# A decode kernel: VectorE and ScalarE given a hardware loop as TensorE has, row sums taken with the exponentials, GpSimd given two layout steps, and the gather and transpose of O moved

## The chip, the cores and the metric

The kernel runs on one core of one Trainium2 chip; the other cores do nothing. The metric is the device time of one execution in microseconds (us), lower is better. Every run named here is of the fast state, and most kernels repeat within about 0.5 us; where one does not, the text says so. Beside each experiment the kernel before was run on the same chip.

## The reference, cut to what matters

The program is one decode step of a gated mix. Branch A is attention over a cache for 8 sequences and 32 heads, branch B a small MLP. All data are bfloat16.

```python
# A: x (8,1,576), k_cache and v_cache (8, 32, 4096, 128), wq (576, 4096), wo (4096, 576)
q = (x @ wq) -> (8, 32, 1, 128)
p = softmax(q . k_cache / sqrt(128))          # over 4096 positions
a = (p . v_cache) -> (8, 1, 4096) @ wo
# B: layernorm, 576 -> 4608, gelu, 4608 -> 576
g = sigmoid(sum(x * gate_w));  return g * a + (1 - g) * b
```

The caches are 537 MB together. With weights 557 MB must be read, and each cache byte is used once.

## The kernel before

The work is cut into 32 groups g, each of one sequence and eight heads. A group needs one K load and one V load of 8.39 MB each (128 partitions with 64 KB each). SBUF holds three such slots, so a load may start when an earlier one has been used up. Per group:

- VectorE multiplies K by q in eight chunks, in place (`mult`); TensorE adds up 16-wide pieces by products with the identity; VectorE reduces what is left (`reduce`).
- VectorE finds the maximum (`softmax`), ScalarE takes the exponentials into P, VectorE adds P up (`rowsum`).
- TensorE multiplies P by V (`pv`), ScalarE copies the result out (`evict`), TensorE gathers it (`gather`), VectorE divides by the sum (`norm`). Every third group TensorE transposes three results (`turn`).

TensorE's groups 2 to 31 are a hardware loop of ten turns with three groups in each. The other engines have all instructions written out. The parts that matter for the argument:

```python
# ... cut: set-up, weights, MLP
    def load_kv(kind, g):                      # one 8.39 MB load, issued from SyncE
        ...
        land[kind, g] = op("sync", lambda e: e.dma_start(slot[s][:, :, :], src), free[n - 3], ...)
# ...
    def rowsum(g):                             # 128x2048 -> 128x1 on VectorE
        v_rs[g] = op("vector", lambda e: e.tensor_reduce(
            out=rr[:, :], in_=P[:, :, :].rearrange("p h t -> p (h t)"), axis=AX.X, op=ALU.add),
            [a_exp[g], p_z.get(g - 1)])
# ...
    for g in range(NG):
        if g >= G0 and place(g) == 0:
            S.mark()                           # a turn of TensorE's loop starts
        def between(c, g=g):                   # called between the eight chunks c of scores(g)
            if g >= G0:
                if c == 1:
                    gather(g - 2)
                if c == 3:
                    norm(g - 2)
                if c == 4 and place(g) == GL - 1:
                    turn((g - 2) // GL)
            if g >= 1 and c == 3:
                rowsum(g - 1)
            if c == 5:
                q_of(g + 1)
        scores(g, between)
        free[n_of["k", g]] = [p_sum[g, NCK - 1]]   # K's slot is free after the last score sum
        next_load()                            # ... the last group loads wo instead
        if g >= 1:
            pv(g - 1)
            free[n_of["v", g - 1]] = [p_pv[g - 1]]
            next_load()
        softmax(g)                             # contains the exponentials
        if g >= 1:
            evict(g - 1)
# ... cut: the last group's O, the product with wo, the output
```

Each freed K slot takes a V load and each freed V slot a K load. The last K slot takes wo.

## Time and profile before

| | before |
|---|---|
| time, median | 1305.18 us (1304.88 to 1305.40, 3 runs) |
| bytes read | 557 MB |
| share of the 16 DMA engines' span used by the load queue | 99.3% |
| VectorE, TensorE, ScalarE busy | 68%, 61%, 12% |
| a cache load lands after the one before | 19.35 us, mostly (433 GB/s) |
| last V lands; last piece of wo lands; end of span | 1287.4; 1298.7; 1302.5 us |

From the profile page of the kernel before: the engines' busy time, share and instructions; the row of DMA shares in 40 slices and the rate in each; then the queues with packets, MB and share of 16 engines' span.

```profile
PE 795.1 (61%) x5186; PEld 355.3 (27%) x5186; DVE 881.6 (68%) x885; ACT 150.0 (12%) x363; POOL 3.4 (0%) x19
DMA  9999999999999999999999999999999999999997
GB/s 393 436 439 419 427 437 433 429 433 435 431 433 433 437 429 441 429 439 431 433 433 423 435 423 443 425 431 439 425 439 429 437 431 423 445 421 441 429 435 297
q1 hardware_dynamic: 11200, 556.93, 99.3%
q14 instruction: 10, 0.08, 0.0%
```

The DMA engines are the resource that is full. Queue 14 brings instructions: only 0.08 MB, whose share rounds to nothing.

From the same page, four groups of instructions (count, busy us, mean ns of one, idle time before them and its cause):

```profile
L503 DVE TENSOR_TENSOR SL<-SL,q_bc 128x4096 bf16<-128x4096 bf16 x256 | 581.7, 2283 | 216.8 <-DMA SL<-in_A_k_cache_dram 216.8
L551 DVE TENSOR_REDUCE rr<-P 128x1 f32<-128x2048 bf16 x32 | 72.9, 2278 | 0.3
L482 ACT ACTIVATE Qm<-Q,sel 128x256 bf16<-128x256 bf16 x33 | 16.3, 495 | 0.0
L511 PE MATMUL psb<-SL,ident 128*128 128x512 bf16 x2048 | 613.6, 459 | 468.1 <-DVE SL L503 467.5
```

VectorE waits 216.8 us for K loads. That is what its slack looks like: the row sums (L551) take 72.9 us of an engine that then waits.

The packet records of the trace give start, duration, size and queue of each DMA packet, but not its engine. As every engine runs almost without a break, a packet belongs to the engine whose last packet ended where it starts. Worked out so, the end of each engine's last cache packet is (us, sorted):

```
before: 1281.7 1281.7 1281.7 1281.7 1281.8 1281.9 1281.9 1282.0 1282.1 1282.1 1282.1 1282.1 1282.3 1282.3 1283.6 1286.9
```

One of the 16 is 5 us behind the typical one. A load counts as landed when all 16 engines have finished their part.

### The profile page before, as it was taken

How to read it: one execution, taken by the hardware profiler on the slowest of the kernel's cores; microseconds unless marked ns; L12 is line 12 of the kernel's file. 1: busy time of each engine (PE TensorE's matmuls, PEld its weight loads, DVE VectorE, ACT ScalarE, POOL GpSimd, SP SyncE). 2: the span in 40 equal slices, each digit the busy share in tenths (PEclk: the TensorE clock that was granted, in tenths of full speed). 3: DMA queues.
4: the chain of work that ended last, by engine and by line, in shares of the span. 5: the costliest groups of instructions: out<-in, count | busy, mean ns of one | idle time of the engine just before them, and what ended most of it. 6: DMA issues, size and time to landing. Idle time of an engine off the chain costs nothing.

```text
span 1302.5 us, 11916 instructions
## 1 busy us (share of the span) xinstructions
PE 795.1 (61%) x5186; PEld 355.3 (27%) x5186; DVE 881.6 (68%) x885; ACT 150.0 (12%) x363; POOL 3.4 (0%) x19
## 2 busy tenths in 40 slices
PE   2467476656667466567557556656557566557556
PEld 1323232223223122223223222223223122223224
DVE  3388577766668576668666667766668676667754
ACT  1011110111110111100111110111110011110011
POOL 1000000000000000000000000000000000000000
PEclk8599786887797787888787797887798788788788
DMA  9999999999999999999999999999999999999997
GB/s 393 436 439 419 427 437 433 429 433 435 431 433 433 437 429 441 429 439 431 433 433 423 435 423 443 425 431 439 425 439 429 437 431 423 445 421 441 429 435 297
DMA packets 11411, 557.27 MB, mean 428 GB/s; under 512 B 1360, under 2 KB 1376, under 8 KB 2816
## 3 DMA queue, kind: packets, MB, share of 16 engines
q1 hardware_dynamic: 11200, 556.93, 99.3%
q8 instruction: 9, 0.15, 0.0%
q10 hardware_dynamic: 192, 0.11, 0.0%
q14 instruction: 10, 0.08, 0.0%
HBM read 557.03 MB, written 0.01 MB: 428 GB/s over the span
## 4 chain that ended last, share of the span: by engine, by line
DMA 55%; DVE 25%; PE 18%; issue 0%; ACT 0%; SPq 0%
DMA SL<-in_A_k_cache_dram 54%; DVE SL L503 18%; PE psb L511 13%; PE psb L565 5%; DVE s_sb L516 4%; DVE rr L551 3%; DMA SL<-in_A_wq_dram 1%; DVE Orow L584 0%; PE psb L403 0%; ACT P L546 0%; PE psb L578 0%; PE psb L454 0%; DVE OT L599 0%; PE psb L593 0%; DVE rz L583 0%
## 5 line engine op out<-in xcount | busy, mean ns | idle before, releaser
L511 PE MATMUL psb<-SL,ident 128*128 128x512 bf16 x2048 | 613.6, 459 | 468.1 <-DVE SL L503 467.5
L503 DVE TENSOR_TENSOR SL<-SL,q_bc 128x4096 bf16<-128x4096 bf16 x256 | 581.7, 2283 | 216.8 <-DMA SL<-in_A_k_cache_dram 216.8
L511 PEld LDWEIGHTS psb<-SL,ident 128*128 128x128 bf16 x2048 | 215.8, 114 | 833.7 <-DVE SL L503 547.3
L516 DVE TENSOR_REDUCE s_sb<-psb 128x32 f32<-128x512 f32 x256 | 175.6, 686 | 109.6 <-PE psb L511 109.4
L546 ACT ACTIVATE P<-s_sb,hb 128x256 bf16<-128x256 f32 x256 | 105.5, 494 | 301.0 <-PE psb L565 255.9
L565 PE MATMUL psb<-SL,P 128*32 128x512 bf16 x2048 | 119.9, 386 | 0.0
L492 ACT ACTIVATE q_bc<-psb 128x128 bf16<-128x128 f32 x32 | 8.9, 278 | 804.4 <-PE psb L486 804.4
L565 PEld LDWEIGHTS psb<-SL,P 128*32 128x32 bf16 x2048 | 91.1, 168 | 28.3 <-issue 13.1
L551 DVE TENSOR_REDUCE rr<-P 128x1 f32<-128x2048 bf16 x32 | 72.9, 2278 | 0.3
L578 PE MATMUL psb<-O_sb,sel 128*8 128x128 f32 x256 | 33.9, 276 | 4.6 <-ACT O_sb L570 4.6
L599 DVE CAST OT<-psb 128x8 bf16<-128x8 f32 x32 | 3.7, 187 | 37.0 <-PE psb L593 37.0
L578 PEld LDWEIGHTS psb<-O_sb,sel 128*8 128x8 f32 x256 | 21.7, 93 | 8.3 <-ACT O_sb L570 4.8
L570 ACT ACTIVATE O_sb<-psb 128x512 f32<-128x512 f32 x32 | 18.4, 575 | 6.0 <-PE psb L565 6.0
L482 ACT ACTIVATE Qm<-Q,sel 128x256 bf16<-128x256 bf16 x33 | 16.3, 495 | 0.0
L425 DVE TENSOR_TENSOR SL<-psb,SL 104x384 f32<-104x384 f32 x3 | 1.7, 553 | 18.7 <-PE psb L421 18.7
L534 DVE TENSOR_REDUCE mA<-s_sb 128x1 f32<-128x256 f32 x32 | 13.4, 420 | 1.1
L444 PE MATMUL psb<-ident,SL 8*32 8x8 bf16 x144 | 8.0, 195 | 7.3 <-DVE SL L435 7.3
L584 DVE TENSOR_SCALAR Orow<-psb,rz 8x128 bf16<-8x128 f32 x32 | 10.9, 340 | 1.1
L583 DVE RECIPROCAL rz<-psb 8x1 f32<-8x1 f32 x32 | 4.8, 149 | 10.1 <-PE psb L578 10.1
L444 PEld LDWEIGHTS psb<-ident,SL 8*32 8x32 bf16 x144 | 7.9, 148 | 7.7 <-DVE SL L435 7.7
L421 PE MATMUL psb<-SL 128*8 128x384 bf16 x60 | 5.0, 475 | 8.0 <-DMA SL<-in_B_w_dram 8.0
L486 PE MATMUL psb<-Qm,Sel 128*64 128x128 bf16 x66 | 8.6, 256 | 0.0
(72 smaller groups left out, 104.8 us busy)
## 6 DMA issues: line engine op xcount, KB each, us to landing
SL<-in_B_w_dram SPq DMA_DIRECT2D x1, 5184.0 KB, 38.4
SL<-in_B_w_dram SPq DMA_DIRECT2D x1, 4608.0 KB, 24.7
SL<-in_A_wq_dram SPq DMA_DIRECT2D x1, 4096.0 KB, 13.1
SL<-in_A_wo_dram SPq DMA_DIRECT2D x1, 2304.0 KB, 11.8
SL<-in_A_wo_dram SPq DMA_DIRECT2D x1, 1152.0 KB, 14.2
SL<-in_B_w_dram SPq DMA_DIRECT2D x1, 576.0 KB, 25.7
SL<-in_A_wo_dram SPq DMA_DIRECT2D x1, 576.0 KB, 15.0
SL<-in_A_wo_dram SPq DMA_DIRECT2D x2, 288.0 KB, 15.3
```

The lines of the kernel that those rows point to most:

```text
L444: p_hT = op("tensor", lambda e, o=o, i=i, c=c: e.matmul(o, lhsT=i, rhs=ident[32 * c:32 * c + B, 32 * c:32 * c + B], start=True, stop=True) ...
L482: t = op("scalar", lambda e: e.activation(out=Qm[:, :, :].rearrange("p k d -> p (k d)"), in_=Q4[:, 2 * hg * DH:(2 * hg + 2) * DH], func=AC ...
L503: v_mult[g, c] = op("vector", lambda e: e.tensor_tensor(out=part, in0=part, in1=qb, op=ALU.mult), [land["k", g], a_qb[g]], token=in_loop(g))
L511: p_sum[g, c] = op("tensor", lambda e, r=r, n=n: e.matmul(tr_ps[par][:, :], lhsT=ident[:, :], rhs=r, start=(n == 0), stop=(n == NCH - 1)), w)
L516: v_red[g, c] = op("vector", lambda e: e.tensor_reduce(out=s_sb[:, s, c * CT:(c + 1) * CT], in_=tr_ps[par][:, :].rearrange("p (t c) -> p t ...
L534: t = op("vector", lambda e: e.tensor_reduce(out=mA[:, 0:1], in_=s_sb[:, s, :], axis=AX.X, op=ALU.max), [v_red[g, NCK - 1], c_mA])
L546: a_exp[g] = op("scalar", lambda e, h=h: e.activation(out=P[:, h, :], in_=s_sb[:, s, :], func=ACT.Exp, bias=hb8[:, h:h + 1], scale=1.0), [ ...
L551: v_rs[g] = op("vector", lambda e: e.tensor_reduce(out=rr[:, :], in_=P[:, :, :].rearrange("p h t -> p (h t)"), axis=AX.X, op=ALU.add), [a_ ...
L565: p_pv[g] = op("tensor", lambda e, o=o, tq=tq: e.matmul(o, lhsT=P[:, :, :].rearrange("p h t -> p (h t)")[:, tq::NTQ], rhs=vb[:, tq::NTQ, : ...
L570: a_ev[g] = op("scalar", lambda e: e.activation(out=O_sb[:].rearrange("p t d -> p (t d)"), in_=o_ps[:, :], func=ACT.Copy), [p_pv[g], p_oz. ...
L578: p_oz[g] = op("tensor", lambda e, tt=tt: e.matmul(oz_ps[0:HB, 0:DH], lhsT=sel32[:, :, tt], rhs=O_sb[:, tt, :], start=(tt == 0), stop=(tt ...
L584: v_norm[g] = op("vector", lambda e: e.tensor_scalar(out=Orow[32 * (g % GL):32 * (g % GL) + HB, :], in0=oz_ps[0:HB, 0:DH], scalar1=rz[0:HB ...
```

## The change: intent and diff

VectorE and ScalarE each get a ten-turn loop like TensorE's, so that they too need no new instructions. The exponentials give their row sums themselves (`accum_out`), so VectorE's row sum goes. GpSimd prepares Qm (the next q, masked, which a product with `Sel` then spreads over the partitions) and places the transposed O. The gather of O, with its sums, and the transpose move to other places in the group, and a V slot is now free only after the eviction. The core of the diff:

```diff
+    LOOPED = ("tensor", "vector", "scalar")
...
+        i0, i1, n, turns = self.body(engine)
         for rec in ops[:i0]:
-            one(rec, False)
-        with eng.Fori(0, (i1 - i0) // n):
-            for rec in ops[i0:i0 + n]:
-                one(rec, True)
+            one(rec)
+        if turns:
+            body, back = self.loops[engine]
+            with eng.Fori(0, turns):
+                for rec, need, give in zip(ops[i0:i0 + n], body, back):
+                    for sem, val in need:
+                        eng.wait_ge(sem, val)
+                    done(rec, rec["fn"](eng))
+                    for sem, by in give:
+                        eng.sem_inc(sem, -by)
         for rec in ops[i1:]:
-            one(rec, False)
+            one(rec)
... (q_of: Qm moves from ScalarE to GpSimd)
-        t = op("scalar", lambda e: e.activation(
-            out=Qm[...], in_=Q4[...], func=ACT.Copy, scale=sel32[...]), ...)
+        g_qm[g] = op("gpsimd", lambda e: e.tensor_scalar(
+            out=Qm[...], in0=Q4[...], scalar1=sel32[...], scalar2=None, op0=ALU.mult), ...)
... (the exponentials give their sums)
+    def exps(g):
         for h in range(HB):
             a_exp[g] = op("scalar", lambda e, h=h: e.activation(
-                out=P[:, h, :], in_=s_sb[:, s, :], func=ACT.Exp, bias=hb8[:, h:h + 1], scale=1.0),
+                out=P[:, h, :], in_=s_sb[:, :], func=ACT.Exp, bias=hb8[:, h:h + 1], scale=1.0,
+                accum_out=acc[:, place(g), h:h + 1]),
...
-    def rowsum(g):
-        v_rs[g] = op("vector", lambda e: e.tensor_reduce(...))
... (the transposed O: one copy on VectorE, then GpSimd)
+    def stage(k):
+        v_st[k] = op("vector", lambda e: e.tensor_copy(out=OTs[:, :, :, :], in_=tp_of), [p_tp[k], g_ot.get(k - 1)])
+    def place_o(k):
+        for g in range(GL * k, min(GL * k + GL, NG)):
+            g_ot[k] = op("gpsimd", lambda e, ...: e.tensor_copy(out=OT[:, 2 * hg:2 * hg + 2, :, b], in_=OTs[:, :, :, g % GL]), [v_st[k]])
... (the order within a group)
-            if g >= G0:
-                if c == 1:
-                    gather(g - 2)
-                if c == 3:
-                    norm(g - 2)
-                if c == 4 and place(g) == GL - 1:
-                    turn((g - 2) // GL)
-            if g >= 1 and c == 3:
-                rowsum(g - 1)
-            if c == 5:
+            if c == 1:
                 q_of(g + 1)
+            if in_loop(g) and place(g) == 0:
+                if c == 2:
+                    turn(k, True)
+                if c == 4:
+                    stage(k)
         scores(g, between)
-        free[n_of["k", g]] = [p_sum[g, NCK - 1]]
+        if in_loop(g):
+            if place(g) == 0 and k >= 0:
+                place_o(k)
+            gather(g - 2)
+        free[n_of["k", g]] = [p_z[g - 2] if in_loop(g) else p_sum[g, NCK - 1]]
...
         if g >= 1:
             pv(g - 1)
-            free[n_of["v", g - 1]] = [p_pv[g - 1]]
-            next_load()
         softmax(g)
+        if in_loop(g):
+            norm(g - 2)
+        exps(g)
         if g >= 1:
             evict(g - 1)
+            free[n_of["v", g - 1]] = [a_ev[g - 1]]
+            next_load()
```

## The prediction

> **What bounds the kernel now: the DMA engines.** The page's queue table puts the load queue at 99.3% of all 16 engines' span, at 428 GB/s on average. The Trainium skill ("DMA: Bandwidth & Descriptors", Specifications) gives a fabric ceiling of 435 GB/s; the landings agree: a typical 8.39 MB cache load lands 19.35 us after the one before, or 433 GB/s. VectorE is 68% busy, TensorE 61%, ScalarE 12%. In the timeline K's slot is given back 6 to 11 us before the load in flight lands, so the queue doesn't run dry: VectorE's 39 us turn has about 11 us of slack.
>
> **What the change removes and adds.** Row sum on VectorE (2.28 us a group, 72.9 us in all): gone. Qm (0.5 us) goes from ScalarE to GpSimd. All inside slack, so worth nothing. A K slot comes back about 2 us sooner; a V slot about 4 us later (after the exps, 3.3 us, and the eviction, 0.58 us), when another 19 us load is still queued behind the one in flight, so that costs nothing either.
>
> **The one thing that reaches the bound: instruction fetch.** Queue 14 in the trace's packet records brings 8192 bytes at 58.8, 238.1, 406.0, 588.1, 778.5, 972.9 and 1145.6 us: about 128 VectorE instructions apart (885 in 1300 us is about 27 a group of 39 us). Each holds up one DMA engine: the next 64 KB packet takes about 3.07 us instead of 2.42, after a 0.3 us gap, so about 0.97 us. The loads landing at 412, 607, 782, 977 and 1152 us indeed came after 20.3 to 20.4 us instead of 19.35. All hit the same engine: at the end 14 of the engines have finished the last V between 1281.7 and 1282.3 us, one only at 1286.9, so V lands at 1287.4 and the last piece of wo at 1298.7. That engine is the critical path.
>
> With VectorE looping, fetches end after the first turn of the loop: the two early ones stay, five go, 5 x 0.97 = 4.8 us, which brings the late engine level with the rest. The Trainium skill ("Runtime: NRT & Kernel Launch", Instruction fetch mechanics) says a taken branch out of the resident pages forces a fetch; but TensorE, which loops already, over a longer body, shows no fetch (queue 8) between 234 and 1295 us. I expect VectorE's shorter body to stay resident too.
>
> Tail: V lands near 1282.6, wo near 1294, the end about 3.8 us later as now. The longer O path (copy on VectorE, then GpSimd) still ends before wo lands.
>
> **Predicted: 1300.3 us (0.4% less), 8 in 10 between 1297.5 and 1305.5.** Faster by over 2%: 0.01 (557 MB at 433 GB/s alone is 1286 us). Within 2%: 0.96. Slower by over 2%: 0.03.
>
> **What would show it.** VectorE busy falls by some 73 us to near 810; row sum lines gone; queue 14 has no packets between about 250 us and the end; the +1 us landings vanish; steady landings stay 19.35 us; queue share stays 99%; last V lands near 1282.6; mean rate near 430 GB/s.
>
> **What would make it wrong.** VectorE's loop refetching pages each turn (one or two fetches in each of 10 turns: same to +12 us); another engine, delayed by TensorE's early fetches or by GpSimd's, becoming the late one, leaving less than 4.8 us; the GpSimd copies or the waits in the tail outlasting wo; a late release of a slot starving the DMA queue.

## The result and the profile after

The changed kernel took 1297.84 us (median of 4, 1297.55 to 1298.07), the kernel before 1305.03 us beside it. The ratio is 0.9945 (95% interval 0.9927 to 0.9962). A ratio here is the mean time of one kernel's fast runs over that of the other's of the same rounds, so not quite the ratio of the medians. Run again later, in another set of runs, the changed kernel took 1297.82 us (1297.69 to 1297.91). The kernel before is less steady: in all rounds it took 1301.8 to 1306.2 us. So the gain is 4 to 8 us, by the run of before that it is set against; in the second set, with the kernel before beside it at 1302.96 us, it was 5.1 us (ratio 0.9958, 0.9944 to 0.9972). It is well under 2%, but outside the spread of both kernels.

From the profile page after: the same rows as before.

```profile
PE 731.7 (56%) x5202; PEld 339.4 (26%) x5202; DVE 804.7 (62%) x833; ACT 160.9 (12%) x587; POOL 40.7 (3%) x82
DMA  9999999999999999999999999999999999999997
GB/s 394 436 433 433 434 433 432 433 431 439 433 433 433 431 439 433 433 433 431 439 429 437 433 431 439 429 437 433 431 437 431 437 433 429 439 431 435 435 429 331
q1 hardware_dynamic: 11200, 556.93, 99.5%
q14 instruction: 4, 0.03, 0.0%
```

Queue 14 has 4 packets in the span instead of 10, and the rate is steadier, near 433 GB/s in most slices, where it swung from 419 to 445. VectorE lost 76.9 us of work (881.6 less 804.7), ten times what the time lost. TensorE's busy time fell by 63 us with almost the same instructions (one score product took 421 ns on average instead of 459, and the mean granted clock was 0.836 instead of 0.818). Neither number explains the gain by itself, as neither engine was the full one.

From the groups after: VectorE's product, the Qm step in its new place, what the sums cost on ScalarE, and TensorE's score product.

```profile
L561 DVE TENSOR_TENSOR SL<-SL,q_bc 128x4096 bf16<-128x4096 bf16 x256 | 581.4, 2281 | 329.6 <-DMA SL<-in_A_k_cache_dram 329.6
L545 POOL TENSOR_SCALAR Qm<-Q,sel 128x256 bf16<-128x256 bf16 x33 | 32.6, 987 | 1030.7 <-ACT O_sb L623 967.1
L606 ACT ACTIVATION_READ_ACCUMULATOR P<-s_sb,hb 128x1 f32 x256 | 47.7, 186 | 0.0
L566 PE MATMUL psb<-SL,ident 128*128 128x512 bf16 x2048 | 550.1, 421 | 519.4 <-DVE SL L561 518.9
```

VectorE's wait for K grew from 216.8 to 329.6 us: it is done sooner and then waits longer. On GpSimd, Qm takes 0.99 us instead of 0.50. Each sum adds an instruction of 0.19 us on ScalarE. All of that lies off the path.

Where the time went can be read from the landings of the cache loads. These are the loads that landed over 0.1 us later than 19.355 us after the one before, from the first K (60.9 and 60.8 us) to the last V, with the excess; then the queue-14 packets' starts; then the end of each engine's last cache packet:

```
before  late: 140.0 +1.67, 256.5 +0.32, 412.3 +0.97, 606.8 +1.01, 761.8 +0.16, 782.3 +1.08, 976.7 +0.96, 1151.9 +0.95; sum 7.12
        queue 14: 59 195 238 406 588 588 779 973 1012 1146 us
after   late: 235.3 +0.39; sum 0.39
        queue 14: 61 153 227 584 us
        ends: 1277.4 1277.9 1277.9 1278.1 1278.3 1278.4 1278.6 1278.7 1278.7 1278.9 1278.9 1279.1 1279.3 1279.3 1279.4 1279.8
```

The last V lands at 1280.3 us instead of 1287.4, 7.1 us sooner; wo follows at 1292.8 instead of 1298.7, and the span ends at 1296.3 instead of 1302.5. The two profiled runs took 1305.04 and 1298.07 us, and their 7.0 us add up so, but for rounding: 7.1 at the last V; 1.2 lost again between V and wo (12.5 us instead of 11.3, for a reason that stays open); 0.2 in the tail; and 0.8 after the span, for the kernel before's time was 2.6 us longer than its span and the changed kernel's 1.8. Two things left the list. One is the row of excesses near 1 us, which follow fetches. The other, 1.67 us at 140 us, follows no fetch of VectorE; it is a part that the prediction did not have. And not only the late engine ended sooner: the other 15 did too, by about 3 us. A missing fetch on one engine cannot do that.

Such loads are issued from SyncE. From the timeline of the kernel before, SyncE alone (start us, duration us, line, what): first the loads after groups 0 and 1, then those of two later groups.

```profile
85.54 0.33 SPq L305 DMA_DIRECT2D SL<-in_A_k_cache_dram  x1
115.44 0.33 SPq L305 DMA_DIRECT2D SL<-in_A_v_cache_dram  x1
...
654.58 0.33 SPq L305 DMA_DIRECT2D SL<-in_A_v_cache_dram  x1
658.25 0.33 SPq L305 DMA_DIRECT2D SL<-in_A_k_cache_dram  x1
697.60 0.33 SPq L305 DMA_DIRECT2D SL<-in_A_v_cache_dram  x1
701.25 0.33 SPq L305 DMA_DIRECT2D SL<-in_A_k_cache_dram  x1
```

And the same view after:

```profile
85.64 0.33 SPq L374 DMA_DIRECT2D SL<-in_A_k_cache_dram  x1
112.74 0.33 SPq L374 DMA_DIRECT2D SL<-in_A_v_cache_dram  x1
...
608.75 0.33 SPq L374 DMA_DIRECT2D SL<-in_A_v_cache_dram  x1
617.74 0.33 SPq L374 DMA_DIRECT2D SL<-in_A_k_cache_dram  x1
```

Each V issue is to be set against the landing of the K load in flight, after which nothing else would be queued. Before: 115.44 against 119.0, a lead of 3.6 us; 654.58 against 664.9, 10.3 us; 697.60 against 703.6, only 6.0 us. In the steady part, the lead before was over 10 us in two groups of three and 6.0 to 7.4 us in the third, which has the transpose in it. After, it was 6.1 us for group 1 and 13.6 us or more from then on (608.75 against 622.3). The K issue now comes 9.0 us behind the V issue instead of 3.7, as the prediction had it, and with a whole V load still queued this costs nothing.

### The profile page after: what moved, and what is told of

Same layout as the page of the kernel before. It is cut to its first block, busy times and chain, and to the rows that moved or that the text cites. A ratio compares the mean times of both kernels' runs of the same rounds, so it can differ in the third digit from the quotient of the medians.

```text
span 1296.3 us, 12332 instructions
## 1 busy us (share of the span) xinstructions
PE 731.7 (56%) x5202; PEld 339.4 (26%) x5202; DVE 804.7 (62%) x833; ACT 160.9 (12%) x587; POOL 40.7 (3%) x82
## 3 DMA queue, kind: packets, MB, share of 16 engines
q1 hardware_dynamic: 11200, 556.93, 99.5%
## 4 chain that ended last, share of the span: by engine, by line
DMA 56%; DVE 25%; PE 13%; ACT 5%; issue 1%; SPq 0%; ACTq 0%
DMA SL<-in_A_k_cache_dram 53%; DVE SL L561 20%; PE psb L566 7%; DVE s_sb L572 5%; ACT P L606 4%; PE psb L617 4%; DMA SL<-in_A_wo_dram 2%; DMA SL<-in_A_wq_dram 1%; PE psb L632 1%; ACT O_sb L623 1%; PE psb L472 0%; SPq L317 0%; PE psb L628 0%; DVE OTs L657 0%; DVE mA L591 0%
## 5 line engine op out<-in xcount | busy, mean ns | idle before, releaser
L566 PE MATMUL psb<-SL,ident 128*128 128x512 bf16 x2048 | 550.1, 421 | 519.4 <-DVE SL L561 518.9
L561 DVE TENSOR_TENSOR SL<-SL,q_bc 128x4096 bf16<-128x4096 bf16 x256 | 581.4, 2281 | 329.6 <-DMA SL<-in_A_k_cache_dram 329.6
L566 PEld LDWEIGHTS psb<-SL,ident 128*128 128x128 bf16 x2048 | 199.7, 106 | 852.8 <-DVE SL L561 612.1
L606 ACT ACTIVATE P<-s_sb,hb 128x256 bf16<-128x256 f32 x256 | 126.3, 494 | 660.8 <-PE psb L617 643.9
L617 PE MATMUL psb<-SL,P 128*32 128x512 bf16 x2048 | 127.0, 386 | 2.8 <-DMA SL<-in_A_v_cache_dram 2.8
L617 PEld LDWEIGHTS psb<-SL,P 128*32 128x32 bf16 x2048 | 95.8, 153 | 20.4 <-DMA SL<-in_A_v_cache_dram 3.3
L545 POOL TENSOR_SCALAR Qm<-Q,sel 128x256 bf16<-128x256 bf16 x33 | 32.6, 987 | 1030.7 <-ACT O_sb L623 967.1
L606 ACT ACTIVATION_READ_ACCUMULATOR P<-s_sb,hb 128x1 f32 x256 | 47.7, 186 | 0.0
L662 POOL COPY OT<-OTs 128x8 bf16<-128x8 bf16 x32 | 5.1, 218 | 219.1 <-DVE OTs L657 219.1
L628 PE MATMUL psb<-ones,acc 128*8 128x1 f32 x64 | 6.3, 167 | 5.3 <-ACT O_sb L623 5.3
## 6 DMA issues: line engine op xcount, KB each, us to landing
SL<-in_A_wq_dram SPq DMA_DIRECT2D x1, 4096.0 KB, 13.6
```

The lines of the kernel that those rows point to most:

```text
L545: g_qm[g] = op("gpsimd", lambda e: e.tensor_scalar(out=Qm[:, :, :].rearrange("p k d -> p (k d)"), in0=Q4[:, 2 * hg * DH:(2 * hg + 2) * DH] ...
L561: v_mult[g, c] = op("vector", lambda e: e.tensor_tensor(out=part, in0=part, in1=qb, op=ALU.mult), [land["k", g], a_qb[g]], token="tensor" ...
L566: p_sum[g, c] = op("tensor", lambda e, r=r, n=n: e.matmul(tr_ps[par][:, :], lhsT=ident[:, :], rhs=r, start=(n == 0), stop=(n == NCH - 1)), ...
L606: a_exp[g] = op("scalar", lambda e, h=h: e.activation(out=P[:, h, :], in_=s_sb[:, :], func=ACT.Exp, bias=hb8[:, h:h + 1], scale=1.0, accum ...
L617: p_pv[g] = op("tensor", lambda e, o=o, tq=tq: e.matmul(o, lhsT=P[:, :, :].rearrange("p h t -> p (h t)")[:, tq::NTQ], rhs=vb[:, tq::NTQ, : ...
```

## The experiments

There were two theories. The **fetch theory** is the prediction's: VectorE's instruction fetches delay one DMA engine, and the slowest engine sets the time; without new fetches the engine is level with the others. The **slot theory**, its rival: VectorE, freed of row sums, gives slots back sooner, and the engines that are ahead don't run dry. All outputs are right.

### 1. VectorE written out again

```diff
-    LOOPED = ("tensor", "vector", "scalar")
+    LOOPED = ("tensor", "scalar")
```

(In this and the next two, a written-out engine waits on the same semaphores by running totals, a change of a few lines in the emitter.)

> The changed kernel, with VectorE's instructions written out again; ScalarE still loops. Fetch theory (each 8192-byte fetch of VectorE's instructions delays one DMA engine by about 0.97 us, and the slowest engine sets the time): queue 14 shows a fetch about every 200 us again, four or five after 230 us, and the time rises by 4 to 5 us, from 1297.8 to 1302 to 1303 us; the loads hit land 1.0 us late. Slot theory (the gain came from VectorE being freed of the row sums, so that slots come back sooner and the DMA engines don't run dry): no change, 1297.8 us.

Measured: 1301.91 us (1301.72 to 1302.10), 4.1 us more than the changed kernel. From its page, queue 14 again:

```profile
q14 instruction: 9, 0.07, 0.0%
```

From its packet records and landings:

```
queue 14: 59 154 241 406 584 601 783 978 1172 us
late: 254.5 +0.11, 410.3 +0.96, 604.8 +0.94, 799.3 +0.96, 993.8 +0.96, 1188.2 +0.97
ends: 1277.5 1277.8 1277.8 1278.0 1278.2 1278.6 1278.6 1278.8 1278.8 1279.0 1279.1 1279.2 1279.3 1279.4 1279.5 1284.5
```

Five fetches came back, each followed by a load 0.94 to 0.97 us late, and a single engine fell behind, to 1284.5 us, while the other 15 ended as in the changed kernel. This is what the fetch theory expected. At such a fetch the next 64 KB packet of that engine starts after a gap of 0.31 us and takes 3.08 us instead of 2.42.

### 2. ScalarE written out again

```diff
-    LOOPED = ("tensor", "vector", "scalar")
+    LOOPED = ("tensor", "vector")
```

> The changed kernel with ScalarE written out, VectorE still looping. Fetch theory: ScalarE's fetches fall on another DMA engine, whose last cache packet ends 1.0 us before the slowest engine's in the changed kernel; at 10 to 12 instructions a group 2 or 3 more fetches, so plus 1 to 2 us, 1299 to 1300 us; if the reading of the row sums counts as instructions of its own, 4 fetches and plus 3 us. Slot theory: 1297.8 us.

Measured: 1298.75 us (1298.75 to 1299.01), 0.9 us more. Four fetches came (386, 658, 927 and 1199 us), about 271 us or 7 groups apart, which is 18 instructions a group at the prediction's 128 a fetch: the reading of sums counts as an instruction of its own. The count of the second branch of the expectation was right, its cost too high: the excess was 0.68 us at the two later loads whose landing this engine set from the start, not 0.97. The engine was 1.0 us ahead of the slowest to begin with. The last V landed 1.9 us later than in the changed kernel, but wo only 0.7: the 1.2 us that the changed kernel loses between V and wo are not lost here, nor in experiments 1 and 6.

### 3. Both written out

```diff
-    LOOPED = ("tensor", "vector", "scalar")
+    LOOPED = ("tensor",)
```

> The changed kernel with VectorE and ScalarE both written out: what the change is worth without its loops. Fetch theory: the fetches fall on two engines and the slower one counts, so the same as with VectorE alone written out, 1302 to 1303 us, and not the sum. Rest of the gain over the kernel before (1305.0) then about 2 us, from group 1's K slot, given back earlier. Slot theory: 1297.8 us.

Measured: 1302.04 us (1301.95 to 1302.15), no more than with VectorE alone written out, though 13 packets ran on queue 14 instead of 9. Fetches on two engines do not add up; the slower engine counts. Both loops together are worth 4.2 us. Without them the changed kernel is much steadier than the kernel before, and a little faster: all four runs lie below the seven of the kernel before beside them (1302.52 to 1304.58), though the interval of the ratio (0.9974 to 1.0007) includes 1.

### 4. The row sum put back on VectorE

```diff
+            if c == 3 and g >= 1:
+                op("vector", lambda e: e.tensor_reduce(
+                    out=rr[:, :], in_=P[:, :, :].rearrange("p h t -> p (h t)"), axis=AX.X, op=ALU.add), [a_exp[g - 1]])
```

> The changed kernel, all loops kept, with the row sum of 128x2048 put back on VectorE in every group (its result unused). Fetch theory: plus 0 to 2 us (only the load after group 1 may land about 1.7 us late, as in the kernel before), 1298 to 1299.8 us, no fetch after 250 us. Slot theory: the gain of 7 us goes, 1304 to 1305 us.

Measured: 1298.72 us (1298.00 to 1299.37), 0.2 to 1.5 us more, and no fetch after 212 us but the one at 589 us that the changed kernel has too (584 us). So the 71 us of VectorE work, as such, is worth no more than that. In the profiled run the load at 140.0 us was 1.52 us late, as in the kernel before; from group 2 on the lead of the V issues stayed at 10.6 us or more, so group 1 is where it cost time.

### 5. One row sum, in group 1 alone

```diff
+            if c == 3 and g == 1:
+                op("vector", lambda e: e.tensor_reduce(
+                    out=rr[:, :], in_=P[:, :, :].rearrange("p h t -> p (h t)"), axis=AX.X, op=ALU.add), [a_exp[g - 1]])
```

> The changed kernel with one extra row sum on VectorE, in group 1 alone. If the 21.03 us landing at 140 us in the kernel before came from group 1's K slot being given back too late, this one instruction of 2.28 us costs about 1.7 us: the first V's successor lands over 20.5 us after the load before it, and the time is 1299.5 us. If not, 1297.8 us.

Measured: 1298.36 us, with a spread of 1297.60 to 1299.91: in some runs it costs nothing, in one 2.1 us. From the profiled run's timeline, SyncE alone:

```profile
85.43 0.33 SPq L375 DMA_DIRECT2D SL<-in_A_k_cache_dram  x1
115.22 0.33 SPq L375 DMA_DIRECT2D SL<-in_A_v_cache_dram  x1
```

The issue is at 115.22 us as in the kernel before (115.44), not at 112.74, and V landed at 139.9 us, 1.66 us late. A single instruction of 2.28 us on an engine with hundreds of us of slack costs up to 2 us, as it sits where the queue is shortest.

### 6. Fetches by an engine that is off the path

```diff
+    idle = sb("idle", [1, 25 * (NG + 1)], mybir.dt.uint8)
...
+        for i in range(25 * g, 25 * g + 25):           # 50 in the second kernel
+            op("gpsimd", lambda e, i=i: e.memset(idle[0:1, i:i + 1], 0))
```

> The changed kernel with 25 one-byte fills a group on GpSimd, whose results nobody reads: some 825 more instructions on an engine off the path, and no wait on them. Fetch theory: 6 more 8192-byte fetches on queue 14, all on one DMA engine that ended 1.4 us ahead of the slowest, so 6 x 0.97 - 1.4 = plus 4.4 us, 1302 us, with VectorE, ScalarE and TensorE unchanged. Slot theory: no change, 1297.8 us.

> As before with 50 fills a group, 1650 more instructions: 12 to 13 more fetches. Fetch theory: 12.5 x 0.97 - 1.4 = plus 10.7 us, 1308.5 us, more than the kernel before. Slot theory: 1297.8 us.

Measured: 1299.55 us (1299.51 to 1299.81) with 25 and 1304.06 us (1303.78 to 1304.21) with 50, that is 1.7 and 6.2 us more. From the page with 50 fills, the engines' row and queue 14:

```profile
PE 730.9 (56%) x5202; PEld 338.7 (26%) x5202; DVE 804.8 (62%) x833; ACT 160.8 (12%) x587; POOL 87.0 (7%) x1732
q14 instruction: 17, 0.14, 0.0%
```

VectorE, ScalarE and TensorE are as in the changed kernel. One-byte fills that nobody reads or waits for cost 6.2 us, by being instructions. The expected counts came, the expected size did not: most loads hit were 0.64 to 0.67 us late, not 0.97, as for ScalarE. With that, the estimate is 12.5 x 0.66 - 1.4 = 6.9 us for 50 fills. Why a fetch of VectorE costs 0.96 us and one of ScalarE or GpSimd 0.66, all of 8192 bytes and all taking about 0.31 us themselves, stays open. The packet after it takes 3.08 us in one case and about 2.8 in the other.

### 7. Two fetching engines at once

VectorE written out (as in 1) and 25 fills a group (as in 6).

> VectorE written out and 25 fills a group on GpSimd: two engines fetch, each through another DMA engine. If the slowest DMA engine counts, the larger of the two single costs: 1302 to 1303 us. If the fetches cost the sum, about 1307 us. Slot theory: 1297.8 us.

Measured: 1301.89 us (1301.87 to 1302.11). The single costs were 4.1 and 1.7 us; together they cost 4.1. The packet ends show why: one engine ended at 1284.8 us, another at 1282.4, the other 14 by 1279.5. Only the last one counts.

### 8. The kernel before, with group 1's row sum moved

```diff
-            if g >= 1 and c == 3:
+            if g >= 2 and c == 3:
                 rowsum(g - 1)
...
         scores(g, between)
+        if g == 1:
+            rowsum(0)
```

> The kernel before with one instruction moved: group 1's row sum (2.28 us on VectorE) runs after that group's last score sum instead of before it, so that K's slot of group 1 is given back 2.3 us sooner; VectorE and ScalarE stay written out. If this slot's late return (3.6 us before the load in flight lands) is what the kernel before loses beside the fetches, the landing at 140 us loses its 1.67 us, and the time falls to 1302.0 us with a narrow spread, as without the new loops. If it was something else, the time stays where the kernel before is on this chip, 1302.5 to 1306 us.

> The changed kernel, unedited, on the same chip: all theories 1297.6 to 1298.1 us. It shows how much the chip matters, since the kernel before has differed by chip and by run (1302.5 to 1306.2 us).

Measured: 1303.41 us (1302.04 to 1304.78, 5 runs), beside 1302.96 us (1301.81 to 1305.05) of the kernel before: no gain that can be told. The excess at 140 us did vanish, and in the profiled run V landed at 1285.6 us, as with no new loops (1285.5). But the spread stayed, the groups with the transpose kept their lead of 5.9 to 7.8 us, and the 15 engines other than the late one ended at 1280.0 to 1281.7 us, not near 1278.5. So group 1 is not all of the rest, and the expectation failed. The unedited changed kernel beside it took 1297.82 us.

The timeline of this run shows one more loss, in the tail. TensorE's last product with V (start, duration; 61 of its 64 products) started 2 us after V had landed, and the last product with wo ended 1.2 us after wo had landed:

```profile
1282.71 3.30 ACT L546 ACTIVATE P<-s_sb,hb 128x256 bf16<-128x256 f32 x8 [38.46 <-PE psb L574]
1285.91 0.57 ACT L570 ACTIVATE O_sb<-psb 128x512 f32<-128x512 f32 x1
1288.02 5.56 PE L565 MATMUL psb<-SL,P 128*32 128x512 bf16 x61
```

The last group's scores ended so late that the exponentials, the eviction of the group before and its gather all came ahead of V's product. Group 31 is one of those with the transpose.

### 9. The kernel before, with all row sums moved

```diff
-            if g >= 1 and c == 3:
-                rowsum(g - 1)
...
         scores(g, between)
+        if g >= 1:
+            rowsum(g - 1)
```

> The kernel before with the row sum of every group moved behind that group's last score sum, VectorE's work and the fetches unchanged. In the kernel before every third group (the one with the turn) issues its V load 6.0 to 7.4 us before the load in flight lands, group 1 3.6 us; the others 10 us and more. Slots come back 2.3 us sooner here, so 8 us and more. If late slots make up the spread and the rest of the gap (1302.0 without the new loops against 1301.8 to 1306.2 us of the kernel before), the time is 1302.0 us with a spread below 0.5 us. If not, 1302 to 1305 us as with only group 1's moved (1302.0 to 1304.8).

Measured: 1302.01 us (1301.77 to 1302.06, 5 runs), beside 1302.47 us (1302.14 to 1304.33). The interval of the ratio (0.9979 to 1.0007) includes 1, but all five runs lie below all nine of the kernel before. This is the time of the changed kernel without its loops (1302.04), with the same narrow spread, and with nothing removed from VectorE: the page has 876.8 us of VectorE work and 10 packets on queue 14.

```profile
PE 750.0 (58%) x5186; PEld 342.3 (26%) x5186; DVE 876.8 (67%) x885; ACT 150.0 (12%) x363; POOL 3.4 (0%) x19
q14 instruction: 10, 0.08, 0.0%
L511 PE MATMUL psb<-SL,ident 128*128 128x512 bf16 x2048 | 564.2, 429 | 509.2 <-DVE SL L503 508.5
```

```
ends: 1277.5 1277.7 1277.8 1278.0 1278.2 1278.2 1278.7 1278.8 1278.9 1279.0 1279.0 1279.1 1279.1 1279.1 1280.0 1284.8
```

The lead of the V issues is 9.9 us and more from group 2 on (group 1: 5.9), and the 15 other engines end as in the changed kernel, about 3 us sooner than in the kernel before. The fetching engine stays behind, and V's last product starts as V lands (1285.4 us). So the spread and the rest of the gap, 0 to 4 us by run, come from the row sum's place ahead of the slot's return, not from its 73 us of work. The slot comes back 3 to 4 us sooner though only 2.28 us were moved: TensorE is faster too (429 ns a score product instead of 459, at a mean granted clock of 0.829 instead of 0.818), and this run does not part the two.

The packet records show where the 15 engines lost their 3 us. From 62 us on, the 64 KB packets took in all 2.7 us an engine longer than 2.42 us each in the kernel before, 0.1 us in the changed kernel and 0.3 us here; from 64 to 1276 us the engines stood idle for 1.1, 0.15 and 0.15 us on average. In the 12 us after the V issue of group 1 (lead 3.6 us) slow packets cost 0.8 us an engine. After those of the groups with the transpose (lead 6.0 to 7.4 us) they cost under 0.1 us until 600 us, and 0.1 to 0.45 us each from 697 us on, when the fetching engine had fallen behind and the others were ahead.

Part of the spread lies outside the span. Of the 32 runs of the kernel before in the experiments' sets, 5 took 2.0 to 3.1 us more than their span, and 2 of the 5 in experiment 8; all other runs of the experiments' sets, of every kernel, took 1.7 to 1.9. One such run is profiled, the kernel before's own: its last packet of queue 8 starts at 1304.3 us, after the span's end, and in every other profile before it. Whether that is the reason was not tested.

### 10. Slots returned late on purpose

```diff
+            if c == 3 and in_loop(g) and place(g) == 2:
+                for i in range(4):
+                    op("vector", lambda e, i=i: e.tensor_reduce(
+                        out=rr[:, i:i + 1], in_=P[:, :, :].rearrange("p h t -> p (h t)"), axis=AX.X, op=ALU.add), [a_exp[g - 1]])
```

> The changed kernel, loops kept, with four row sums (9.1 us of VectorE) in every third group of the loop: their V load is issued about 4.6 us before the load in flight lands, where the changed kernel has 13.7 us. No fetch is added. If a late slot costs by itself, as at group 1 (3.6 us, 1.6 us lost), each of the ten loses some tenths of a microsecond up to 1 us, plus 2 to 10 us in all, 1300 to 1308 us, and the spread of the runs grows. If only fetches count, 1297.8 us.

Measured: 1303.81 us (1302.93 to 1305.42), 6.0 us more, without any added fetch. The time is inside the range, but mostly for a reason that was not meant. In nine of the ten groups the lead of the V load fell to 3.8 to 4.7 us (the tenth, group 31, gives its slot to wo), and in the profiled run all engines ended between 1279.9 and 1281.4 us instead of 1277.4 to 1279.8; yet V landed only 1.6 us later (1281.9) and wo 0.9 us (1293.7). The rest of the 5.7 us of span is tail: group 31 is one of the ten, so V's last product started 6 us after V had landed, and the span ended 8.3 us after wo instead of 3.5.

```profile
1288.49 5.46 PE L618 MATMUL psb<-SL,P 128*32 128x512 bf16 x61
1298.91 0.37 DVE L759 SCALAR_TENSOR_TENSOR out_sb<-psb,g,bmg_sb 104x144 bf16<-104x144 f32 x1 [1.27 <-PE psb L524]
```

In the changed kernel these two started at 1280.34 and 1293.18 us:

```profile
1280.34 5.16 PE L617 MATMUL psb<-SL,P 128*32 128x512 bf16 x64 [2.81 <-DMA SL<-in_A_v_cache_dram]
1293.18 0.37 DVE L753 SCALAR_TENSOR_TENSOR out_sb<-psb,g,bmg_sb 104x144 bf16<-104x144 f32 x1 [2.11 <-PE psb L523]
```

So it shows that a late slot and a late last group each cost time with no fetch involved. The run's time does not give the price of a late slot by itself; the packet records do: in the 12 us after each of the nine V issues, slow packets cost 0.13 to 0.44 us an engine.

No version beat the changed kernel. What an even spread of delays over the 16 engines would still give is small: its slowest engine ends at 1279.8 us, the median one at 1278.7.

## Why the prediction was right, and where its sum was off

The direction, the bound and the main mechanism were right, and the time of 1297.84 us is in the range (1297.5 to 1305.5), but only 0.3 us above its lower end: that it held is partly luck, as one term was left out. The gain forecast was 4.9 us against 7.2 measured; the 5.1 us of the second set are close to it because the kernel before took less time there.

- **"What bounds the kernel now: the DMA engines."** Right. 76.9 us less VectorE work and 63 us less TensorE time left the steady landing at 19.35 us. The load queue's share went from 99.3% to 99.5%.
- **"five go, 5 x 0.97 = 4.8 us".** Right. Written out, VectorE brings five late landings of 0.94 to 0.97 us back (experiment 1), and both new loops are worth 4.2 us of time (experiment 3). The last V landed 4.8 us later without VectorE's loop, but wo only 3.5 us.
- **"I expect VectorE's shorter body to stay resident too."** Right: no fetch of VectorE shows between 227 us and the end.
- **"queue 14 has no packets between about 250 us and the end".** Wrong by one packet, at 584 us. It stays there (584 to 589 us) with either loop written out and with row sums put back, and with fills on GpSimd it is one of the regular row that they bring (197, 391, 586, 777 us). The 64 KB packet after it took 2.77 us, as after the fills' fetches (2.77), where it is 2.80 after ScalarE's and 3.08 after VectorE's. So it is probably GpSimd's, which now has 82 counted instructions instead of 19. No load landed late after it.
- **"All inside slack, so worth nothing", of the row sum, and "so the queue doesn't run dry".** This is the step that failed, and the reason for the larger gain: the term was put at 0 and measured 0 to 4 us by run, 3 us against the runs that the prediction started from (1305.0 less 1302.0). The lead of 6 to 11 us was read from the steady part. It missed group 1, with 3.6 us. It also took "not dry" from the landing, which the slowest engine sets; the other engines are up to 5 us ahead, and for them a lead of 6 us is by this estimate 1 us. Experiment 9 shows that moving the row sums alone, with no work removed, recovers this term, and in its packet records where it was lost. Of the 3 us, 0.8 lie outside the span.
- **"Tail: ... the end about 3.8 us later as now."** Nearly right: 3.5 us after wo. In the profiled run of experiment 8 the last group's own work held the end up, to 4.4 us after wo. V and wo themselves landed at 1280.3 and 1292.8 us, not near 1282.6 and 1294, by the step that failed. How much of the kernel before's spread is late slots, the tail, or time after the span is open, as only one run of each set is profiled; all go when the row sums move.
- **"one engine ... brings the late engine level with the rest".** Right, but the rest moved too, from about 1282 to about 1278.5 us, for the reason just given.

## What to carry to other kernels

Where DMA engines are full, ask of each engine separately when it ends: a few kilobytes on one of sixteen cost as much as if all had waited, and costs on different ones don't add. Instructions count too, even those of an engine that idles; a hardware loop for each long instruction stream, or fewer instructions, takes its fetches away. And work on an engine with slack is free only while the buffers still come back early enough. Here leads of 10 us and more cost nothing that shows, while one of 3.6 us did, and those of 6 to 8 us did once one engine had fallen behind. Behind the instruction that gives a buffer back such work was free: order it there before trying to remove it.

## What the Trainium skill lacked or had wrong

- "Runtime: NRT & Kernel Launch", Instruction fetch mechanics, has refills of 16 KiB blocks and calls the cost of crossing a block "mostly hidden". Here TensorE's refills were 16384 bytes (queue 8), but VectorE's, ScalarE's and GpSimd's were 8192 (queue 14). Beside full DMA engines, a refill of VectorE delayed one DMA engine by 0.94 to 0.97 us, and the time by as much when that engine was the last; one of ScalarE or GpSimd mostly by 0.64 to 0.68 us.
- The same section says that runtime control flow is expensive and that kernels prefer full unrolling. Here loops on VectorE and ScalarE saved 4.2 us (1302.04 to 1297.84). The case that the page gives as its reason, a branch out of the resident pages, did not arise: no fetch of VectorE or ScalarE shows after the loop's first turn, with three groups in the body.
- "DMA: Bandwidth & Descriptors", in its note on iDMA beside load streams (section SWDGE vs HWDGE vs iDMA), says within an explanation marked unconfirmed that a bulk load runs at the pace of its slowest engine. The runs agree, but no page looked at says that a few instruction fetches are enough to let one engine drift 5 us behind within a kernel (last cache packet at 1286.9 us against 1281.7 to 1282.3 for 14 of the others).
